# Larger clusters for the low-rank term: 12 token tiles at a time, with a second layout of V for two batches

## The chip, the cores and the metric

The kernel runs on one core of one Trainium2 chip. The metric is the device time of one execution in microseconds (us). The kernel before the change took 324.93 us (median of 3 runs, 324.88 to 324.94).

Engine names below: PE is TensorE's matmul side and PEld its weight load, DVE is VectorE, ACT is ScalarE, POOL is GpSimd, SP is SyncE, which here only issues DMAs. "L457" is line 457 of the kernel.

## What is computed

`x` has 8 batches of 4224 tokens with 192 channels. First a causal convolution of 7 taps along the tokens, with softmaxed taps per head (8 heads of 24 channels). On its result y a mixer block works:

```python
xt = x.transpose(0, 2, 1)                 # x is now the convolution's result, y
h = xt @ U @ V                            # rank 32, along the tokens
u = x + h.transpose(0, 2, 1)
ch = np.maximum(u @ w_ch1, 0.0) @ w_ch2   # 192 -> 768 -> 192
return (u + ch).astype(np.float32)
```

U is 4224 x 32 and V is 32 x 4224. All matrix work is done in bf16 with float32 sums.

## The kernel before

**Tiles and groups.** A token tile is 128 tokens. A batch has 33 tiles, so there are 264; eight tiles make a group, and there are 33 groups (`GT = 8`, `NG = 33`). As 33 is odd, the first tile of batches 1, 3, 5 and 7 has an odd number when tiles are counted through all batches. A group may hold tiles of two batches.

**The stages.**
- `conv32` (L321): the convolution of one batch as banded matmuls, a head at a time into two PSUM banks, evicted to `y_sb` by ACT and DVE (L256, L258). It reads x and a shifted copy `xb_sb` that POOL makes (`x_shift`, L293 to L305).
- `tt_mm`, `tt_split`, `tt_sum` (L396 to L435): the 32 x 192 product of U and y for one batch, in one PSUM bank. `tt_split` takes it out as a high part (`tt_hi`, ACT, L416) and a low part (`tt_lo`, DVE, L417), `tt_sum` adds up the column groups with two matmuls (L428) and DVE writes `tt_sb` (L422), copied into all four 32-partition row groups.
- `h_tiles` (L446): for a stretch of tiles of one batch, one matmul a tile (L457) of 32 rows of V by `tt_sb`, and on DVE the add u = y + h (L479). Tiles 2·pr and 2·pr+1 share one PSUM bank, and their matmul uses row group pr % 4. All matmuls of the first halves of the banks are issued first, then all of the second halves. One add covers both tiles of a bank if they lie in the same half group of four; otherwise there are two adds (L470). `h_group` (L488) calls this for the eight tiles of a group.
- `transp` (L496): the DMA transpose of a group of u into `uT`, issued on SP.
- `w1` (L542): a group's first product, 36 matmuls (L554) in 6 blocks of two banks, each block evicted with relu into `rl_sb` by ACT (L568) or DVE (L570). 
- `w2` (L577): two tiles' second product, 12 matmuls (L583) into one bank; DVE adds u and writes `out_sb` (L592), and SP sends it out (L600). There are four such pieces a group.

**PSUM.** All PSUM tiles come from one pool of eight banks (`psp`, `bufs=8`, one tag), taken in turn by `bank()` (L56). The banks for h are taken in the order in which `h_tiles` first meets them.

**The order of the work** is written by hand in `SLOTS` (L619 to L668), and every engine works through its own instructions in that order. A slot does w1 of its groups, then their w2 pieces, numbered p = 0, 1, ...; before piece p it does what `at[p]` lists: `c` a part of a convolution, `x` the shifted copy for the next batch, `t` and `s` the two steps of the U product, `h10` the h of group 10 and its transpose. Slots k = 5 to 13 come from a loop: each has three groups (12 pieces), and makes h for three groups further on, at p = 5, 8 and 11 (k = 5 to 9, where batch k-2 is convolved as well) or at p = 0, 4 and 8 (k = 10 to 12). In the profile, the slots with k = 5 to 13 begin at 81.16, 109.46, 137.40, 165.57, 193.59, 221.61, 246.48, 271.44 and 296.04 us.

**Loads.** x of batch b comes in four POOL DMAs during w1 (`x_load`, L610), with steps of `x_shift` between them (L794 to L806). V lies in `V_sb` (L711): partition block q holds tile pairs q, q+4, and so on; it is loaded by five POOL DMAs near the start (L715, L722).

Of the kernel before, what the change touches and what calls it, by code (L numbers as in the profile page):

```python
# [9 lines left out]
BF16 = mybir.dt.bfloat16  # L10
# [4 lines left out]
def kernel(  # L15
# [10 lines left out]
    nc = tc.nc  # L26
    P = nc.NUM_PARTITIONS
    B, S, D = x.shape
    H, KC = weight.shape
    GS = D // H  # L30
    R = moe_U.shape[1]
    M4 = moe_w_ch1.shape[1]
    NT = S // P
    MC = M4 // P
    assert (D, R, MC, S % P) == (192, 32, 6, 0)
    GT = 8
    NTT = B * NT
    NG = NTT // GT
# [6 lines left out]
    cst = ctx.enter_context(tc.tile_pool(name="cst", bufs=1))  # L45
# [10 lines left out]
    def bank():  # L56
        return psp.tile([P, 512], F32, name="ps", tag="ps")
# [45 lines left out]
    def iota(t, pattern, base, mul):  # L103
# [20 lines left out]
        out=Ur[:, 0:nfull, :], in_=U4[0 : nfull * P, :].rearrange("(k p) c -> p k c", p=P)  # L124
# [10 lines left out]
    for m0, m1 in ((0, 2 * P), (2 * P, M4)):  # L135
        for hf in range(2):
            nc.gpsimd.dma_start(
                out=W1_sb[HB * hf : HB * hf + HB, :, m0:m1],
                in_=moe_w_ch1[:, m0:m1].rearrange("(c k) m -> k c m", k=HB),
# [27 lines left out]
    for hh in range(2):  # L167
# [3 lines left out]
        out=dif[:], in0=dif[:], scalar1=rq[:, 0:1], scalar2=None, op0=ALU.add  # L171
# [5 lines left out]
        out=d_sb[:],  # L177
# [8 lines left out]
        out=hot[:],  # L186
# [6 lines left out]
        out=ident[:], in0=fp[:], scalar1=float(P), scalar2=None, op0=ALU.is_equal  # L193
# [9 lines left out]
        out=c_sb[:].rearrange("p k h -> p h k"),  # L203
# [5 lines left out]
    for hh in range(2):  # L209
        pr = sml.tile([P, KC, HQ, BW], BF16, name="pr")  # L210
        prs.append(pr)
        nc.vector.tensor_tensor(
            out=pr[:],
# [8 lines left out]
        out=Eq[:], in0=efp[:], scalar1=rq[:, 1:2], scalar2=None, op0=ALU.is_equal  # L222
# [3 lines left out]
        out=fp[:], in0=fp[:], scalar1=R - 1, scalar2=None, op0=ALU.bitwise_and  # L226
# [3 lines left out]
        out=R4[:], in0=fp[:], scalar1=0.0, scalar2=None, op0=ALU.is_equal  # L230
# [181 lines left out]
    def tt_split(b, p):  # L412

        hi = sml.tile([P, D], BF16, name="tt_hi")
        lo = sml.tile([P, D], BF16, name="tt_lo")
        nc.scalar.activation(out=hi[:], in_=p[:, 0:D], func=ACT.Copy)  # L416
        nc.vector.tensor_tensor(out=lo[:], in0=p[:, 0:D], in1=hi[:], op=ALU.subtract)  # L417
        ttb[b] += [hi, lo]
# [22 lines left out]
    def u_group(g):  # L441
        if ut[g] is None:
            ut[g] = us.tile([P, 4, 3, 2, HB], BF16, name="u_sb")
        return ut[g]

    def h_tiles(b, j0, j1):  # L446

        banks = {}
        for a in range(2):
            for pr in range(j0 // 2, (j1 + 1) // 2):  # L450
                j = 2 * pr + a
                if not j0 <= j < j1:
                    continue
                q = pr % 4
                if pr not in banks:
                    banks[pr] = bank()
                nc.tensor.matmul(  # L457
                    out=banks[pr][:, a * D : (a + 1) * D],
                    lhsT=V_sb[32 * q : 32 * q + 32, (j // 8) * 2 + j % 2, :],
                    rhs=ttb[b][32 * q : 32 * q + 32, :],  # L460
                    start=True,
                    stop=True,
                    tile_position=(32 * q, 0),
                )
        for pr in sorted(banks):
            js = [j for j in (2 * pr, 2 * pr + 1) if j0 <= j < j1]
            runs = []
            for j in js:
                t = b * NT + j
                if runs and t % 4 != 0:  # L470
                    runs[-1].append(j)
                else:
                    runs.append([j])
            for run in runs:
                n = len(run)
                t = b * NT + run[0]
                g, hf, i = t // GT, (t % GT) // 4, t % 4
                a = run[0] % 2
                nc.vector.tensor_tensor(  # L479
                    out=u_group(g)[:, i : i + n, :, hf, :],  # L480
                    in0=yt[b][:, run[0] : run[0] + n, :].rearrange("p n (c k) -> p n c k", c=3),
                    in1=banks[pr][:, a * D : (a + n) * D].rearrange(
                        "p (n c k) -> p n c k", n=n, c=3
                    ),
                    op=ALU.add,
                )

    def h_group(g):  # L488
        t0, t1 = g * GT, g * GT + GT
        while t0 < t1:  # L490
            b = t0 // NT
            te = min(t1, (b + 1) * NT)
            h_tiles(b, t0 - b * NT, te - b * NT)
            t0 = te

    def transp(g):  # L496
        uTt[g] = uts.tile([P, 4, 3, P], BF16, name="uT")
        return nc.sync.dma_start_transpose(
            out=uTt[g][:].rearrange("p i c t -> p (i c) t"),
            in_=ut[g][:].rearrange("p i c f k -> p (i c f k)"),  # L500
        )
# [100 lines left out]
    def held(ins, after):  # L602
        tc.add_manual_dep(
            ins.ins,
            after.ins.name,
            mybir.DependencyInfo(mybir.DependencyClass.Sync, mybir.DependencyReason.DATA),
            reason="transfer held back",
        )

    def x_load(b, q, after):  # L610
        if q == 0:
            x_tile(b)
            x_zero(b, nc.gpsimd)
        held(x_part(b, *XP[q]), after)
# [4 lines left out]
    SLOTS = [  # L619
        ([0], [], {}),  # L620
        ([1], [0], {0: ["h0"], 1: ["h3", "l2:2"], 2: ["l2:3"]}),
        ([2], [1], {0: ["d1", "h1"], 1: ["t1"], 3: ["s1"], 4: ["h4", "x2:6"]}),
        ([3], [2], {1: ["h5"], 3: ["h6"]}),
        (
            [4, 5],
            [3, 4, 5],
            {
# [8 lines left out]
            },  # L636
        ),
    ]
    nh = 10
    for k in range(5, 14):  # L640
        gs = list(range(3 * k - 9, 3 * k - 6))
        hs = [f"h{g}" for g in range(nh, min(nh + 3, NG))] + [None] * 3
        nh = min(nh + 3, NG)
        if k == 5:
            at = {
                2: ["c3:0:3:AAD"],
                3: ["c3:3:3:AAD"],
                4: ["c3:6:2:A", "x4:4"],
                5: [hs[0]],
                6: ["t3"],  # L650
                8: ["s3", hs[1]],
                11: [hs[2]],
            }
        elif k < 10:
            b = k - 2
            at = {
                0: [f"c{b}:0:2:A"],
                2: [f"c{b}:2:3:AAD"],
                3: [f"c{b}:5:3:AAD"] + ([f"x{b + 1}:4"] if b + 1 < B else []),
                5: [f"t{b}", hs[0]],  # L660
                7: [f"s{b}"],
                8: [hs[1]],
                11: [hs[2]],
            }
        else:
            at = {0: [hs[0]], 4: [hs[1]], 8: [hs[2]]}
        SLOTS.append((gs, gs, {p: [w for w in what if w] for p, what in at.items()}))
    assert nh == NG  # L668

    LOADS = {2: [(1, 5), (1, 5)], 3: [(4, 1), (4, 4), (5, 1), (5, 4)]}  # L670
    for b in range(4, B):
        g = 3 * b - 6
# [25 lines left out]
    o = 0  # L698
    for r, (k0, k1) in KP[2].items():
        j = NB0 // 2 * r + k0  # L700
        nc.gpsimd.tensor_copy(
            out=U4_sb[:, o : o + k1 - k0, :, :],
            in_=U_sb[:]
# [6 lines left out]
    NSL = (NT + 7) // 8 * 2  # L710
    V_sb = cst.tile([P, NSL, P], BF16, name="V_sb")  # L711
    full = NT // 8
    for q in range(4):
        src = moe_V[:, 0 : full * 8 * P].rearrange("r (k q t) -> r k q t", q=4, t=2 * P)
        nc.gpsimd.dma_start(  # L715
            out=V_sb[32 * q : 32 * q + 32, 0 : 2 * full, :].rearrange(
                "r (k a) t -> r k (a t)", a=2
            ),
            in_=src[:, :, q, :],
# [3 lines left out]
        out=V_sb[0:32, 2 * (NT // 8), :], in_=moe_V[:, (NT - 1) * P : NT * P]  # L723
# [32 lines left out]
    for r in range(4):  # L756
        q = slice(QB * r, QB * r + QB)
        for hh in range(2):
            nc.gpsimd.tensor_copy(
                out=band2[q, HQ * hh : HQ * hh + HQ, :],  # L760
                in_=bands[hh][q, :, HB * (r % 2) : HB * (r % 2) + QB],
            )

    def do(what):
        if what[0] == "c":
            b, h0, n, engs = what[1:].split(":")
            conv32(int(b), int(h0), int(n), engs)
            return
        if what[0] == "d":
            for h in range(H):  # L770
                last = conv(int(what[1:]), h, 1, [0, 1], "AA" if h == 2 else "AD")
            held(transp(3), last)
            return
        if what[0] == "l":
            b, q = (int(v) for v in what[1:].split(":"))
            x_load(b, q, done_w2[-1])
            return
        if what[0] == "x":
            b, n = (int(v) for v in what[1:].split(":"))
            steps.extend(x_shift(b))  # L780
            for _ in range(n):
                steps.pop(0)()
            return
        n = int(what[1:])
        if what[0] == "h":
            h_group(n)
            if n > 1 and n != 3:
                transp(n)
        elif what[0] == "t":
            tt_split(n, tt_mm(n, range(NT)))  # L790
        else:
            tt_sum(n)

    for gs1, gs2, at in SLOTS:  # L794
# [13 lines left out]
        for p in range(npc + 1):  # L808
            for what in at.get(p, []):
                do(what)  # L810
            if p < npc:
                g, k = gs2[p // 4], p % 4
# [35 lines left out]
```

## Time and profile before

| what | value |
|---|---|
| median of 3 runs | 324.93 us |
| span of the profiled execution, first to last instruction | 323.2 us |
| TensorE clock granted | 1.00 of full speed |
| busy: PE, DVE, ACT, POOL | 317.6, 268.6, 170.0, 142.7 us |
| L583 (w2) matmuls | 141.2 us busy, 1584 |
| L554 (w1) matmuls | 131.7 us busy, 1188 |
| L457 (h) matmuls | 12.4 us busy, 264 |
| L479 (u = y + h) on DVE | 168 adds: 96 of two tiles, mean 547 ns, and 72 of one tile, mean 347 ns |

The page is of one execution; its own time is the span and what lies around it, and the median is 1.7 us above the span. Matmuls are pipelined: the time of one (246 ns for L583) is longer than the distance between two starts, and the distances are what add up. The "chain" is the work that ended last, followed back from the end: at each step to what released an instruction, or to the one before it on its engine. A timeline row gives the start, the length and the engine; `x12` says that twelve instructions were merged, and square brackets tell how long the engine was idle before and for whom.

### The profile page before, as it was taken

What the parts mean: (1) busy time and instruction counts of PE and PEld (TensorE: products, weight loads), DVE (VectorE), ACT (ScalarE), POOL (GpSimd) and SP (SyncE); (2) the same over time, 40 slices, a digit from 0 to 9 for tenths busy, and PEclk for the clock granted to TensorE, in tenths of its full rate; (3) what the DMA queues carried; (4) which work ended last, traced back from release to release, by engine and by line L of the source; (5) the groups of instructions that cost most, each with busy time, mean ns of one, the idle gap of its engine ahead of it and who ended that gap; (6) DMA issues with size and microseconds to landing.
All of it is one profiled execution on the core that took longest, in us unless ns stands there. A gap on an engine that the chain in (4) does not pass through costs nothing.

```text
span 323.2 us, 9583 instructions
## 1 busy us (share of the span) xinstructions
PE 317.6 (98%) x3996; PEld 223.7 (69%) x3996; DVE 268.6 (83%) x551; ACT 170.0 (53%) x344; POOL 142.7 (44%) x111
## 2 busy tenths in 40 slices
PE   8999999999999999999999999999999999999995
PEld 3747676478677647866864884687797497487495
DVE  6769989987977986997898699789888897896863
ACT  1766724860874397088239609824903902912910
POOL 8764179728957983992897497000000000000000
PEclk9999999999999999999999999999999999999999
DMA  9999993999998999599499957138268059048035
GB/s 106 192 191 183 206 209 100 196 192 257 208 135 200 246 142 190 166 189 209 130 237 192 181 149 194 52 105 231 61 178 262 3 150 275 18 121 271 2 121 173
DMA packets 122906, 53.51 MB, mean 166 GB/s; under 512 B 87760, under 2 KB 122832, under 8 KB 122864
## 3 DMA queue, kind: packets, MB, share of 16 engines
q1 hardware_dynamic: 84528, 38.08, 45.4%
q0 software_dynamic: 38192, 14.73, 39.2%
q8 instruction: 31, 0.51, 0.7%
q10 hardware_dynamic: 144, 0.10, 0.1%
q14 instruction: 11, 0.09, 0.1%
HBM read 29.49 MB, written 25.95 MB: 172 GB/s over the span
## 4 chain that ended last, share of the span: by engine, by line
PE 92%; ACT 3%; DMA 2%; DVE 1%; issue 0%; POOL 0%; POOLq 0%
PE ps L583 42%; PE ps L554 39%; PE ps L339 3%; PE ps L457 3%; DMA x_sb<-in_x_dram 2%; PE ps L402 2%; ACT rl_sb L568 2%; PE ps L369 1%; ACT y_sb L256 1%; PE ps L509 1%; DVE u_sb L479 1%; DVE rl_sb L570 1%; PE ps L524 0%; PE ps L428 0%; POOL x_sb L79 0%
## 5 line engine op out<-in xcount | busy, mean ns | idle before, releaser
L568 ACT ACTIVATE rl_sb<-ps 128x512 bf16<-128x512 f32 x233 | 124.3, 604 | 108.0 <-PE ps L554 96.0
L583 PE MATMUL ps<-W_sb,rl_sb 128*128 128x192 bf16 x1584 | 141.2, 246 | 0.2
L583 PEld LDWEIGHTS <-rl_sb 128*128 128x128 bf16 x1584 | 128.3, 98 | 11.8 <-issue 11.5
L554 PE MATMUL ps<-uT,W_sb 64*128 64x512 bf16 x1188 | 131.7, 376 | 0.0
L570 DVE TENSOR_SCALAR rl_sb<-ps 128x512 bf16<-128x512 f32 x163 | 105.3, 688 | 15.7 <-PE ps L554 15.4
L554 PEld LDWEIGHTS <-W_sb 64*128 64x128 bf16 x1188 | 66.9, 94 | 60.4 <-issue 3.9
L592 DVE TENSOR_TENSOR out_sb<-ps,u_sb 128x384 f32<-128x384 f32 (+1 forms) x133 | 70.4, 551 | 25.5 <-PE ps L583 25.0
L305 POOL COPY xb_sb<-x_sb 32x3072 bf16<-32x3072 bf16 (+1 forms) x24 | 67.4, 2824 | 0.5
L479 DVE TENSOR_TENSOR u_sb<-y_sb,ps 128x192 bf16<-128x192 bf16 (+1 forms) x168 | 66.3, 461 | 0.0
L293 POOL COPY xb_sb<-x_sb 128x3072 bf16<-128x3072 bf16 x12 | 32.7, 2742 | 42.1 <-PE ps L339 32.2
L256 ACT ACTIVATE y_sb<-ps 128x384 bf16<-128x384 f32 (+4 forms) x90 | 38.3, 520 | 9.7 <-PE ps L339 7.4
L79 POOL DMA_DIRECT2D x_sb<-in_x_dram x32 | 27.0, 848 | 9.6 <-PE ps L457 3.8
L258 DVE CAST y_sb<-ps 128x408 bf16<-128x408 f32 (+4 forms) x36 | 19.1, 578 | 1.3 <-PE ps L369 1.0
L457 PE MATMUL ps<-tt_sb,V_sb 32*128 32x192 bf16 x264 | 12.4, 246 | 0.1
L339 PE MATMUL ps<-x_sb,band 64*32 64x384 bf16 x192 | 12.1, 333 | 0.0
L339 PE MATMUL ps<-xb_sb,band 64*32 64x384 bf16 x192 | 12.1, 332 | 0.0
L457 PEld LDWEIGHTS <-V_sb 32*128 32x128 bf16 x264 | 4.7, 92 | 7.3 <-issue 7.3
L416 ACT ACTIVATE tt_hi<-ps 128x192 bf16<-128x192 f32 x8 | 2.6, 330 | 11.9 <-PE ps L402 11.9
L369 PE MATMUL ps<-x_sb,band 64*64 64x240 bf16 (+3 forms) x192 | 8.0, 276 | 0.2 <-DMA x_sb<-in_x_dram 0.2
L339 PEld LDWEIGHTS <-band 64*32 64x32 bf16 x384 | 4.5, 89 | 5.2 <-issue 2.4
L153 PE MATMUL ps<-zz 128*128 128x512 f32 (+1 forms) x10 | 6.7, 816 | 1.1 <-DVE zz L143 1.1
L369 PEld LDWEIGHTS <-band 64*64 64x64 bf16 x192 | 6.0, 106 | 2.1 <-issue 1.4
(65 smaller groups left out, 71.3 us busy)
## 6 DMA issues: line engine op xcount, KB each, us to landing
out_dram<-out_sb SPq DMA_DIRECT2D x131, 192.0 KB, 2.7
x_sb<-in_x_dram POOLq DMA_DIRECT2D x14, 384.0 KB, 6.9
x_sb<-in_x_dram POOLq DMA_DIRECT2D x7, 432.0 KB, 6.7
x_sb<-in_x_dram POOLq DMA_DIRECT2D x7, 408.0 KB, 8.0
x_sb<-in_x_dram POOLq DMA_DIRECT2D x1, 504.0 KB, 7.3
uT<-u_sb SPq DMA_TRANSPOSE x31, 3.5
x_sb<-in_x_dram POOLq DMA_DIRECT2D x1, 480.0 KB, 5.6
W_sb<-in_moe_w_ch_dram POOLq DMA_DIRECT2D x2, 192.0 KB, 7.8
```

What stands on the lines that cost most here:

```text
L79: return nc.gpsimd.dma_start(out=xt[b][HB * r : HB * r + HB, s0:s1, :], in_=x[b, blk * HB : (blk + s1 - s0) * HB, :].rearrange("(j p) d -> ...
L256: nc.scalar.activation(out=out, in_=in_, func=ACT.Copy)
L293: nc.gpsimd.tensor_copy(out=xbt[b][:, s0:s1, :], in_=xt[b][:, s0 + 1 : s1 + 1, :])
L305: nc.gpsimd.tensor_copy(out=xbt[b][q, s0:s1, :], in_=xt[b][q, s0:s1, :])
L339: nc.tensor.matmul(out=pp[r][QB * cg : QB * cg + QB, 0 : nk[r] * GS], lhsT=w[hr], rhs=t[hr, st : st + 2 * nk[r] - 1 : 2, hs], start=True, ...
L457: nc.tensor.matmul(out=banks[pr][:, a * D : (a + 1) * D], lhsT=V_sb[32 * q : 32 * q + 32, (j // 8) * 2 + j % 2, :], rhs=ttb[b][32 * q : 32 ...
L479: nc.vector.tensor_tensor(out=u_group(g)[:, i : i + n, :, hf, :], in0=yt[b][:, run[0] : run[0] + n, :].rearrange("p n (c k) -> p n c k", c=3),
L554: last = nc.tensor.matmul(out=pps[m][hf][:], lhsT=W1_sb[HB * hf : HB * hf + HB, c, m * P : (m + 1) * P], rhs=uTt[g][HB * hf : HB * hf + HB ...
L568: nc.scalar.activation(out=rl[:, m, hf, :], in_=pp[hf][:], func=ACT.Relu)
L570: nc.vector.tensor_scalar_max(out=rl[:, m, hf, :], in0=pp[hf][:], scalar1=0.0)
L583: last = nc.tensor.matmul(out=cps[:, a * D : (a + 1) * D], lhsT=rlt[g][:, m, hf, (i + a) * P : (i + a + 1) * P], rhs=W2_sb[:, m, :], start ...
L592: nc.vector.tensor_tensor(out=o[:, 0:n, :].rearrange("p n (c k) -> p n c k", c=3), in0=cps[:, 0 : n * D].rearrange("p (n c k) -> p n c k", ...
```

## The change

For k = 5 to 12, h is no longer made group by group but for stretches of tiles (`w80:92` is tiles 80 to 91), two stretches a slot: 12 and 12 tiles (k = 5 to 9), or 10 and 12 (k = 10 to 12, as far as tiles are left). They stand at p = 5 and 9 (k = 6 to 9), at 6 and 10 (k = 5), and at 0 and 6 (k from 10). After a stretch, the groups that it completes are transposed. For batches 5 and 7, V is read from a second layout `Vo_sb` in which tiles 2·pr-1 and 2·pr stand together, so that a bank holds two tiles which lie in the same half group. `Vo_sb` is loaded by six POOL DMAs in slot k = 6, listed at p = 8, which POOL meets behind the four steps of `x5:4`.

```diff
     def h_tiles(b, j0, j1):
+        o, V = (1, Vo_sb) if b in odd else (0, V_sb)
         banks = {}
         for a in range(2):
-            for pr in range(j0 // 2, (j1 + 1) // 2):
-                j = 2 * pr + a
+            for pr in range((j0 + o) // 2, (j1 + o + 1) // 2):
+                j = 2 * pr + a - o
...
-                    lhsT=V_sb[32 * q : 32 * q + 32, (j // 8) * 2 + j % 2, :],
+                    lhsT=V[32 * q : 32 * q + 32, (pr // 4) * 2 + a, :],
...
-            js = [j for j in (2 * pr, 2 * pr + 1) if j0 <= j < j1]
+            js = [j for j in (2 * pr - o, 2 * pr + 1 - o) if j0 <= j < j1]
...
-    nh = 10
+    nt = 10 * GT
     for k in range(5, 14):
         gs = list(range(3 * k - 9, 3 * k - 6))
-        hs = [f"h{g}" for g in range(nh, min(nh + 3, NG))] + [None] * 3
-        nh = min(nh + 3, NG)
+        hs = []
+        for n in (12, 12) if k < 10 else (10, 12):
+            hs.append([f"w{nt}:{min(nt + n, NTT)}"] if nt < NTT else [])
+            nt = min(nt + n, NTT)
         if k == 5:
...
-                5: [hs[0]],
-                6: ["t3"],
-                8: ["s3", hs[1]],
-                11: [hs[2]],
+                6: ["t3"] + hs[0],
+                8: ["s3"],
+                10: hs[1],
...
-                5: [f"t{b}", hs[0]],
+                5: [f"t{b}"] + hs[0],
                 7: [f"s{b}"],
-                8: [hs[1]],
-                11: [hs[2]],
+                9: hs[1],
             }
+            if k == 6:
+                at[8] = ["v"]
         else:
-            at = {0: [hs[0]], 4: [hs[1]], 8: [hs[2]]}
+            at = {0: hs[0], 6: hs[1]}
...
+    odd = (5, 7)
+    Vo_sb = cst.tile([P, NSL, P], BF16, name="Vo_sb")
+
+    def v_odd():
+        for q in range(4):
+            k0 = 1 if q == 0 else 0
+            c0 = (8 * k0 + 2 * q - 1) * P
+            nk = full - k0
+            nc.gpsimd.dma_start(
+                out=Vo_sb[32 * q : 32 * q + 32, 2 * k0 : 2 * full, :].rearrange(
+                    "r (k a) t -> r k (a t)", a=2
+                ),
+                in_=bass.AP(
+                    tensor=moe_V.tensor,
+                    offset=moe_V.offset + c0,
+                    ap=[[S, R], [8 * P, nk], [1, 2 * P]],
+                ),
+            )
+        nc.gpsimd.dma_start(out=Vo_sb[0:32, 1, :], in_=moe_V[:, 0:P])
+        nc.gpsimd.dma_start(
+            out=Vo_sb[0:32, 2 * full : 2 * full + 2, :].rearrange("r a t -> r (a t)"),
+            in_=moe_V[:, (NT - 2) * P : NT * P],
+        )
...
+        if what == "v":
+            v_odd()
+            return
+        if what[0] == "w":
+            t0, t1 = (int(v) for v in what[1:].split(":"))
+            h_span(t0, t1)
+            for g in range(t0 // GT, t1 // GT):
+                transp(g)
+            return
```

`h_span(t0, t1)` is the loop of `h_group` over the batches that a stretch touches, with the ends given.

More of the change, by code (lines that the diff above doesn't have):

```diff
@@ L477, in h_tiles @@
                 g, hf, i = t // GT, (t % GT) // 4, t % 4
-                a = run[0] % 2
+                a = (run[0] + o) % 2
                 nc.vector.tensor_tensor(
@@ L486, in h_tiles, with h_span @@
                 )
-    def h_group(g):
-        t0, t1 = g * GT, g * GT + GT
+    def h_span(t0, t1):
         while t0 < t1:
@@ L494, in h_group @@
             t0 = te
+    def h_group(g):
+        h_span(g * GT, g * GT + GT)
     def transp(g):
@@ L659 @@
                 3: [f"c{b}:5:3:AAD"] + ([f"x{b + 1}:4"] if b + 1 < B else []),
-                5: [f"t{b}", hs[0]],
+                5: [f"t{b}"] + hs[0],
                 7: [f"s{b}"],
-                8: [hs[1]],
-                11: [hs[2]],
-            }
-        else:
-            at = {0: [hs[0]], 4: [hs[1]], 8: [hs[2]]}
-        SLOTS.append((gs, gs, {p: [w for w in what if w] for p, what in at.items()}))
-    assert nh == NG
+                9: hs[1],
+            }
+            if k == 6:
+                at[8] = ["v"]
+        else:
+            at = {0: hs[0], 6: hs[1]}
+        SLOTS.append((gs, gs, at))
+    assert nt == NTT
     LOADS = {2: [(1, 5), (1, 5)], 3: [(4, 1), (4, 4), (5, 1), (5, 4)]}
```

## The prediction

> **What bounds the kernel now.** I read the page's parts 1 and 4 first, then the chain in order of time, then the timelines of TensorE (PE), VectorE (DVE) and GpSimd (POOL) in one slot.
>
> ```profile
> PE 317.6 (98%) x3996; PEld 223.7 (69%) x3996; DVE 268.6 (83%) x551; ACT 170.0 (53%) x344; POOL 142.7 (44%) x111
> ...
> PE 92%; ACT 3%; DMA 2%; DVE 1%; issue 0%; POOL 0%; POOLq 0%
> ```
>
> PE is 92% of the chain: what is taken from PE's stream is gained, and what PE waits for is lost. DVE, at 83%, has little room to be late. Slot k=8 of the plan (165.57 to 193.59) shows a stretch that the change rewrites. PE's timeline there; the first number is when the first matmul of a group starts:
>
> ```profile
> 184.35 0.92 PE L402 MATMUL ps<-y_sb,U_sb 128*32 128x192 bf16 x33
> 185.20 0.34 PE L457 MATMUL ps<-tt_sb,V_sb 32*128 32x192 bf16 x8
> 185.48 2.15 PE L583 MATMUL ps<-W_sb,rl_sb 128*128 128x192 bf16 x24
> ...
> 187.63 1.15 PE L583 MATMUL ps<-W_sb,rl_sb 128*128 128x192 bf16 x12
> 188.72 0.42 PE L457 MATMUL ps<-tt_sb,V_sb 32*128 32x192 bf16 x8
> 189.07 3.14 PE L583 MATMUL ps<-W_sb,rl_sb 128*128 128x192 bf16 x36
> 192.15 0.34 PE L457 MATMUL ps<-tt_sb,V_sb 32*128 32x192 bf16 x8
> ```
>
> There is no idle time: each group follows the last. DVE in the same stretch, also without a gap after its first row:
>
> ```profile
> 185.67 0.36 DVE L417 TENSOR_TENSOR tt_lo<-ps,tt_hi 128x192 bf16<-128x192 f32 x1 [0.65 <-ACT tt_hi L416]
> 185.94 1.94 DVE L479 TENSOR_TENSOR u_sb<-y_sb,ps 128x384 bf16<-128x384 bf16 x4
> 187.80 1.02 DVE L592 TENSOR_TENSOR out_sb<-ps,u_sb 128x384 f32<-128x384 f32 x2
> 188.73 0.35 DVE L422 CAST tt_sb<-ps 128x192 bf16<-128x192 f32 x1
> 188.99 0.55 DVE L592 TENSOR_TENSOR out_sb<-ps,u_sb 128x384 f32<-128x384 f32 x1
> 189.46 2.00 DVE L479 TENSOR_TENSOR u_sb<-y_sb,ps 128x384 bf16<-128x384 bf16 x5
> 191.38 1.48 DVE L592 TENSOR_TENSOR out_sb<-ps,u_sb 128x384 f32<-128x384 f32 x3
> ```
>
> From the distances of the starts, DVE takes 0.465 for an add of two tiles or an output add (a result is ready 0.55 after its start), 0.26 for an add of one tile or a tt row (ready after 0.35).
>
> Does PE ever wait for such adds? Yes, in slot k=4, in the chain:
>
> ```profile
> 65.23 0.83 DVE u_sb L479 x3
> ...
> 66.22 1.08 DVE u_sb L479 x3
> ...
> 258.24 0.45 PE ps L457 x8
> ```
>
> All PSUM tiles come from one ring of eight banks, so an allocation waits for the reader of the one eight before it. In slot 4 the convolution's matmuls wait for the h adds. The last row (slot 11, right behind w1) is a cluster of 0.45 instead of 0.28: its fifth bank is held by a ScalarE relu that ends at 258.40 in ScalarE's timeline, and the matmul goes at 258.45. I take release = end of the reader + 0.05.
>
> **The change, part by part.**
>
> *Matmuls and breaks.* Eight tiles take 0.28 (185.20 to 185.48) or 0.35 (188.72 to 189.07). The matmuls of a cluster use four row groups, and one that needs a busy row group waits 0.08: counting the tiles of each group in the order of issue gives two waves for the 0.28 and three for the 0.35. Groups 10 to 32 are 23 clusters, four of them of three waves (12, 16, 20, 24): 23 x 0.28 + 4 x 0.08 = 6.76. Afterwards there are 16: 15 of four waves (0.44; six prs on four row groups, twice) and one of six (tiles 188 to 199, 0.60): 7.20. Loss 0.44. A w2 run cut in two costs 0.10 (12 matmuls alone 1.09, 36 take 3.08, so 0.995 per piece plus 0.10). Clusters that cut a run by themselves, and do not stand beside w1, tt or an earlier cut: 16 before, 8 after. Gain 0.80. Together -0.36.
>
> *DVE adds.* Carrying line 470's rule through both plans: 65 adds of two tiles and 54 of one become 81 and 22. 16 x 0.465 - 32 x 0.26 = -0.9 of DVE work. That is off the chain; it counts only through the banks. The old backlog into w1 is shorter too: slot 7's w1 is 11.92 against 11.76 elsewhere. -0.16.
>
> *Banks, slot 8, carried by hand.* First cluster, tiles 152 to 163: six banks, 185.20 to 185.64. Then p5 and p6 (1.99), s (0.16), p7 and p8 (2.08): the second cluster starts at 189.87. DVE: six adds 185.94 to 188.73, p5 188.73, p6 189.20, tt_sb 189.66, p7 189.92, p8 190.39, next adds 190.86. The second cluster, tiles 164 to 175, needs seven banks: eight allocations back lie three of the first cluster's, then p5, p6, s, p7. The seventh is p7's, free at 189.92 + 0.55 + 0.05 = 190.52. Its matmul stands in the middle: one more wave and the leaving (0.17) put the end at 190.78, not 190.31: **wait 0.47**. The next piece, p9, needs p8's bank: 190.39 + 0.60 = 190.99, **0.21** more. Slot 8: 0.68.
>
> The others by the same carry. Slot 5 (six banks, then seven): 0.68. Slot 6 (seven, then seven): p5 now takes the bank of tt, which tt_lo releases at 186.08 in slot 8's clock, while PE is there at 185.64: 0.44; three paired and six single adds take 2.96, so p7's bank comes at 190.69 and p8's at 191.16, against a cluster from 190.31: 0.20 + 0.21. Total 0.85. Slot 7 (seven, six): 0.44. Slot 9 (six, six): p9 waits 0.05. Sum 2.70. Before, all of these were zero: an 8-tile cluster has four or five banks, and the piece eight back had always been read.
>
> *Slots 10 to 12.* The first cluster stands right behind w1, with five or six banks. The fifth comes 0.275 after the start (258.17 to 258.45) instead of 0.08: 3 x 0.19. In slot 11 six banks are taken and the next piece needs that of the last relu, which ends at 258.89: 0.77 after the start against 0.63: 0.14. Before, slots 11 and 12 waited 0.17 and 0.19. Net +0.35.
>
> The Trainium skill pulls both ways here ("TensorEngine Tiling (Array Packing)"). Its section "Key Properties" says that a change of tiling mode drains TensorE: by that alone fewer clusters gain, as the -0.36 has it. Its "PSUM Pressure" says that row tiles write to different banks and that software must keep them apart, which speaks against seven banks at once: by that the +3.05 decides. The trace shows both prices, and the second is larger.
>
> *Vo and POOL.* Six more POOL DMA issues in slot 6, behind four x_shift steps. The nearest rows, V's own loads on line 715, take 0.54 each, and line 722's took 0.51: 4 x 0.54 + 2 x 0.51 = 3.2, with gaps 3.5. Queued behind them are x_load of batch 6 and the last two steps of x_shift(5), for which slot 7's first convolution (149.25) waits.
>
> ```profile
> 137.87 0.17 POOL L74 MEMSET x_sb<- 64x96 uint32 x1
> 138.49 0.82 POOL L79 DMA_DIRECT2D x_sb<-in_x_dram  x1 [0.45 <-PE ps L554]
> ...
> 142.85 3.08 POOL L305 COPY xb_sb<-x_sb 32x3456 bf16<-32x3456 bf16 x1
> ```
>
> The last step ends at 145.93. With 3.5 more, less the 0.45 that POOL sat idle, plus slot 5's delay (0.68 less about 0.25 of gains): 149.4. PE, itself late by slots 5 and 6 (1.53 less some 0.5 of gains), comes at 150.3. Cover 0.9: cost zero. If an issue takes as long as x's (0.82 to 0.86 each), some 1.7 more, PE waits about 0.8. The loads also add 0.27 MB written to DMA engines that are about full in slots 5 to 8; x of batch 6 lands later, by some 5 us at worst, and the cover in slot 8 (POOL done at 174.1, convolution at 177.26) shrinks to about one. Bounds: 0 to +1.2; I take 0, since V's rows are the same shape. On SP two transposes now stand together (1.44 each) before the outputs of p9 to p11; eight output buffers hold them through w1. Zero. Moving the second cluster to p9 leaves its groups at least a w1 pair (7.8) before use. Zero.
>
> Sum: -0.36 - 0.16 + 2.70 + 0.35 = **+2.5**. The profiled execution has a span of 323.2; the median of 324.93 lies 1.7 outside it, in what the change does not touch. 324.93 + 2.5 = **327.4**.
>
> **Rivals.** 1. *The banks come free in time* (not slower): if DVE ran some 0.9 ahead of my carry at p9 and the tt bank were free at p5, none of the 2.70 would arise and the late 0.35 stays at most; what remains is -0.36 - 0.16, about -0.5: 324.4. It decides from the point where p7's bank is free before the second cluster. For it: only the releases' order is inferred, not seen, in slots 5 to 9. Against it: slot 4's rows and slot 11's. 2. *POOL's cover is lost*: +1.2 on top, 328.6; for it, the full DMA engines. 3. *The second layout does not pair as meant* in batches 5 and 7: slot 9 would wait like slot 6 (0.85, not 0.05), and slots 11 and 12 some 0.3 for a further bank: +1.1, 328.5; against it, the index arithmetic gives 16 pairs in one bank each.
>
> **Chances.** Forecast 0.72, rival 1 0.13, rival 2 0.12, rival 3 0.03. The measurement tells about 0.2%, 0.65 us, from no change. Rival 1 lies within that, with a tail below: 0.09 of it same and 0.04 faster; 0.02 of the forecast's own chance is same, where the waits nearly vanish; the rest, 0.85, is slower. Range: the waits at half (1.5 of 3.05) give +1.0, 325.9, and I go a little below; rivals 2 and 3 reach 328.6. So 325.7 to 328.7; left out are rival 1 and a few hundredths at each end.
>
> **What would show it.** Right: in the chain after, u_sb L479, out_sb L592 and tt_lo L417 or waits of PE appear in w2 of slots 5 to 8 and hardly in 9; clusters of 12 at 0.44 where they do not wait; w2 runs unchanged between cuts; 152 adds on L479 instead of 168 (49 of the slots before 5, and 103). Wrong: the w2 parts of slots 5 to 8 no longer than before (rival 1), x_sb or xb_sb in the chain at slot 7's or 8's first convolution (rival 2), or clusters of 12 that take much more or less than 0.44.

## The result, and the profile after

The kernel after the change takes 327.15 us (median of 22 runs, 326.81 to 331.13) against 325.12 for the kernel before in the same rounds (22 runs). The ratio is 1.0065, with a 95% interval of 1.0046 to 1.0085; the medians differ by 2.0 us. The forecast was 327.4.

What follows rests on the traces. "Body" is the time from the first w1 matmul of slot 5 to the end of the last output add, "end" what follows up to the last instruction. The body leaves out the first 81 us, which the change does not touch and whose length moves by some 0.6 from execution to execution. Each body and each end is of one profiled execution. A slot that an edit does not touch agrees between kernels within 0.05; the one exception is slot 5 of e9.

| slot | before | after | difference |
|---|---|---|---|
| 5 | 28.30 | 28.73 | +0.42 |
| 6 | 27.94 | 28.75 | +0.80 |
| 7 | 28.17 | 28.30 | +0.14 |
| 8 | 28.02 | 28.55 | +0.53 |
| 9 | 28.02 | 28.09 | +0.06 |
| 10 | 24.87 | 24.90 | +0.03 |
| 11 | 24.96 | 25.04 | +0.08 |
| 12 | 24.60 | 24.89 | +0.29 |
| body (with slot 13) | 239.10 | 241.45 | +2.35 |
| end | 3.02 | 2.80 | -0.22 |

The page after, parts 1 and 4 (L480 is now the add of u, L557 and L586 the matmuls of w1 and w2, L595 the output add):

```profile
PE 318.0 (98%) x3996; PEld 220.4 (68%) x3996; DVE 268.5 (82%) x535; ACT 170.0 (52%) x344; POOL 146.1 (45%) x117
...
PE 85%; DVE 6%; ACT 4%; DMA 3%; issue 1%; POOL 0%; POOLq 0%
```

PE is 85% of the chain instead of 92%, and DVE 6% instead of 1%. PE's busy share is still 98%, so the busy share does not show the loss. PE's timeline in slot 8 does:

```profile
186.78 0.50 PE L458 MATMUL ps<-tt_sb,V_sb 32*128 32x192 bf16 x12
187.22 2.15 PE L586 MATMUL ps<-W_sb,rl_sb 128*128 128x192 bf16 x24
...
191.45 0.25 PE L458 MATMUL ps<-tt_sb,V_sb 32*128 32x192 bf16 x1
191.45 0.43 PE L458 MATMUL ps<-tt_sb,Vo_sb 32*128 32x192 bf16 x5
192.11 0.34 PE L458 MATMUL ps<-tt_sb,Vo_sb 32*128 32x192 bf16 x6 [0.23 <-DVE out_sb L595]
192.57 3.13 PE L586 MATMUL ps<-W_sb,rl_sb 128*128 128x192 bf16 x36
```

The first cluster of 12 takes 0.44 (186.78 to 187.22). The second takes 1.12 (191.45 to 192.57). Half way, six matmuls stand still for an output add on DVE. DVE there:

```profile
187.52 2.87 DVE L480 TENSOR_TENSOR u_sb<-y_sb,ps 128x384 bf16<-128x384 bf16 x6
190.31 1.02 DVE L595 TENSOR_TENSOR out_sb<-ps,u_sb 128x384 f32<-128x384 f32 x2
191.24 0.35 DVE L422 CAST tt_sb<-ps 128x192 bf16<-128x192 f32 x1
191.50 1.01 DVE L595 TENSOR_TENSOR out_sb<-ps,u_sb 128x384 f32<-128x384 f32 x2
```

Six adds hold DVE for 2.8; the output adds of p5 to p8 follow without a gap. p7's starts at 191.50 and ends 0.55 later, and the waiting matmul goes at 192.11. In slots 6 and 7, PE waits at once behind the first cluster; in slot 7:

```profile
158.48 0.50 PE L458 MATMUL ps<-tt_sb,V_sb 32*128 32x192 bf16 x12
159.36 2.14 PE L586 MATMUL ps<-W_sb,rl_sb 128*128 128x192 bf16 x24 [0.38 <-DVE tt_lo L417]
```

Seven banks are taken, so the next piece needs the bank of tt, which tt_lo still reads: 0.88 from cluster to piece instead of 0.44.

### The profile page after: what moved, and what is told of

The parts are those of the page before. It is cut to its first block, busy times and chain, and to the rows that moved or that the text cites. A ratio compares the mean times of both kernels' runs of the same rounds, so it can differ in the third digit from the quotient of the medians.

```text
span 325.6 us, 9583 instructions
## 1 busy us (share of the span) xinstructions
PE 318.0 (98%) x3996; PEld 220.4 (68%) x3996; DVE 268.5 (82%) x535; ACT 170.0 (52%) x344; POOL 146.1 (45%) x117
## 4 chain that ended last, share of the span: by engine, by line
PE 85%; DVE 6%; ACT 4%; DMA 3%; issue 1%; POOL 0%; POOLq 0%
PE ps L557 38%; PE ps L586 37%; PE ps L339 3%; DVE u_sb L480 3%; ACT rl_sb L571 2%; DMA x_sb<-in_x_dram 2%; DVE out_sb L595 2%; PE ps L458 2%; PE ps L402 2%; PE ps L369 1%; ACT y_sb L256 1%; PE ps L512 1%; DMA out_dram<-out_sb 1%; DVE rl_sb L573 1%; PE ps L527 0%
## 5 line engine op out<-in xcount | busy, mean ns | idle before, releaser
L586 PE MATMUL ps<-W_sb,rl_sb 128*128 128x192 bf16 x1584 | 139.8, 246 | 1.5 <-DVE tt_lo L417 0.8
L586 PEld LDWEIGHTS <-rl_sb 128*128 128x128 bf16 x1584 | 129.2, 98 | 11.6 <-issue 10.9
L557 PE MATMUL ps<-uT,W_sb 64*128 64x512 bf16 x1188 | 131.5, 376 | 0.0
L557 PEld LDWEIGHTS <-W_sb 64*128 64x128 bf16 x1188 | 61.2, 94 | 66.0 <-issue 3.1
L595 DVE TENSOR_TENSOR out_sb<-ps,u_sb 128x384 f32<-128x384 f32 (+1 forms) x133 | 70.0, 551 | 26.0 <-PE ps L586 25.6
L480 DVE TENSOR_TENSOR u_sb<-y_sb,ps 128x384 bf16<-128x384 bf16 (+1 forms) x152 | 64.7, 494 | 0.0
L458 PE MATMUL ps<-tt_sb,V_sb 32*128 32x192 bf16 x198 | 10.1, 246 | 0.4 <-DVE out_sb L595 0.2
```

The lines of the kernel that those rows point to most:

```text
L458: nc.tensor.matmul(out=banks[pr][:, a * D : (a + 1) * D], lhsT=V[32 * q : 32 * q + 32, (pr // 4) * 2 + a, :], rhs=ttb[b][32 * q : 32 * q + ...
L480: nc.vector.tensor_tensor(out=u_group(g)[:, i : i + n, :, hf, :], in0=yt[b][:, run[0] : run[0] + n, :].rearrange("p n (c k) -> p n c k", c=3),
L557: last = nc.tensor.matmul(out=pps[m][hf][:], lhsT=W1_sb[HB * hf : HB * hf + HB, c, m * P : (m + 1) * P], rhs=uTt[g][HB * hf : HB * hf + HB ...
L586: last = nc.tensor.matmul(out=cps[:, a * D : (a + 1) * D], lhsT=rlt[g][:, m, hf, (i + a) * P : (i + a + 1) * P], rhs=W2_sb[:, m, :], start ...
L595: nc.vector.tensor_tensor(out=o[:, 0:n, :].rearrange("p n (c k) -> p n c k", c=3), in0=cps[:, 0 : n * D].rearrange("p (n c k) -> p n c k", ...
```

## The experiments

All times are medians in us with the number of runs; the ratio is to the kernel before in the same rounds, with its 95% interval. The first row is of the first rounds; in the later ones the kernel before took 325.10 (with e2, e4, e6) and 325.16 (with e8, e9, e10).

| kernel | median (runs) | ratio | body | end |
|---|---|---|---|---|
| before | 325.12 (22) | 1 | 239.10 | 3.02 |
| after | 327.15 (22) | 1.0065 (1.0046 to 1.0085) | 241.45 | 2.80 |
| e1: no second layout | 329.43 (4) | 1.0121 (1.0089 to 1.0153) | 242.42 | 3.85 |
| e2: groups of eight, second layout | 324.57 (12) | 0.9978 (0.9956 to 1.0001) | 238.83 | 2.79 |
| e3: h before the U product | 329.02 (4) | 1.0120 (1.0065 to 1.0175) | 241.84 | 2.81 |
| e4: late clusters one piece later | 326.86 (12) | 1.0049 (1.0020 to 1.0077) | 241.09 | 2.80 |
| e5: second cluster later | 327.80 (6) | 1.0078 (1.0054 to 1.0102) | 241.73 | 2.80 |
| e6: groups placed by banks | 325.86 (12) | 1.0013 (0.9994 to 1.0032) | 238.82 | 3.77 |
| e7: four output pieces by ACT | 326.15 (10) | 1.0033 (1.0008 to 1.0057) | 240.27 | 2.81 |
| e8: e3, and s later | 325.86 (12) | 1.0012 (0.9992 to 1.0032) | 240.02 | 2.79 |
| e9: e6 with the second layout | 324.63 (12) | 0.9989 (0.9953 to 1.0024) | 239.17 | 2.80 |
| e10: before, four more DVE instructions | 326.43 (12) | 1.0041 (1.0013 to 1.0069) | 239.14 | 3.93 |

The diffs are against the kernel after, except for e10.

### e1: the stretches without the second layout

```diff
-                at[8] = ["v"]
+                pass
...
-    odd = (5, 7)
+    odd = ()
```

> Three theories for the 2.0 us that the change costs. Banks: PE waits for PSUM banks that DVE reads late. Load: the six loads of the second layout, on POOL and on full DMA engines. Waves: a cluster of 12 is dearer on PE by itself. Here the stretches stay and the second layout goes, with its loads. Banks: slot 9 then has seven banks in both clusters and should wait like slot 6 (0.89 in the trace after the change, instead of 0.06), slots 11 and 12 some 0.2 more for a further bank: about +1.0 on the changed kernel, 328.2. Load: the 2.0 go, 325.1. Waves: 327.1, or a little less, since fewer waves are needed at the end.

The body is 0.97 longer than after the change, where the banks asked for about 1.0. Slot 9 goes from +0.06 to +0.72 against the kernel before, slot 11 from +0.08 to +0.35. Slot 9 now has seven banks in both clusters:

```profile
215.23 0.50 PE L458 MATMUL ps<-tt_sb,V_sb 32*128 32x192 bf16 x12
216.11 2.14 PE L586 MATMUL ps<-W_sb,rl_sb 128*128 128x192 bf16 x24 [0.38 <-DVE tt_lo L417]
```

This cluster takes 0.88 up to the next piece, and so does the second (220.33 to 221.21). The loads are not what the change costs: without them the kernel is slower. The median moved by 2.3, more than the body: the end is 3.85 instead of 2.80. That was not in any theory, and e10 takes it up.

### e2: the second layout without the stretches

```diff
-        for n in (12, 12) if k < 10 else (10, 12):
+        for n in (8, 8, 8):
...
-                6: ["t3"] + hs[0],
-                8: ["s3"],
-                10: hs[1],
+                5: hs[0],
+                6: ["t3"],
+                8: ["s3"] + hs[1],
+                11: hs[2],
...
-                9: hs[1],
+                8: hs[1],
+                11: hs[2],
...
-                at[8] = ["v"]
+                at[8] = at[8] + ["v"]
...
-            at = {0: hs[0], 6: hs[1]}
+            at = {0: hs[0], 4: hs[1], 8: hs[2]}
```

> The other half of the change alone: groups of eight at their old places, with the second layout for batches 5 and 7 and its six loads. Banks: no cluster has more than five banks, nothing waits that did not before, DVE has a little less to do and the small waits at the starts of slots 10 to 12 shrink: 0 to 0.4 below the kernel before. Load: 2.0 above it, 327.1. Waves: as before.

The body is 0.27 shorter than before, mostly in slot 12 (-0.19, no bank wait behind w1); slot 8 is 0.07 shorter and slot 9 0.08 longer, which has to do with row groups (see the part on why the prediction was right). The median is 0.5 lower, and 0.2 of that is the end; the interval of the ratio still touches 1. The loads cost nothing that shows, the second layout is a small gain, and the loss of the change lies in the stretches.

### e7: output pieces evicted by ACT

```diff
-        nc.vector.tensor_tensor(
...
+        if 6 <= g < 21 and g * 4 + t0 // 2 - 12 * (g // 3) in (5, 6, 7, 8):
+            nc.scalar.activation(
+                out=o[:, 0:n, :].rearrange("p n d -> p (n d)"),
+                in_=cps[:, 0 : n * D],
+                func=ACT.Copy,
+            )
+        else:
+            nc.vector.tensor_tensor(
...
```

> The output pieces p = 5 to 8 of slots 5 to 9 are copied out of PSUM by ACT, without the addition of u, which is left out for these 20 pieces; everything else stays. ACT is idle there. Banks: what the second cluster waits for (the banks of pieces 5 to 8 and the adds behind which DVE reads them) is free at once: 0.69 + 0.45 + 0.69 + 0.06 = 1.9 less, 325.2; the 0.45 at the tt bank in slots 6 and 7 stay. Load and waves: 327.1.

The body is 1.18 shorter than after the change, with the same matmuls and the same loads. So the lateness of DVE's reads is the larger part of what PE waited for in the second clusters. I expected 1.9, and 0.7 stayed: 0.28 in slot 5 and 0.21 each in slots 6 and 8. In slot 5 the second cluster stands at p = 10, so the piece behind it needs the bank of p9, which DVE still read. Slot 8 shows what stayed with ACT:

```profile
190.51 0.50 PE L458 MATMUL ps<-tt_sb,Vo_sb 32*128 32x192 bf16 x11
191.16 1.07 PE L586 MATMUL ps<-W_sb,rl_sb 128*128 128x192 bf16 x11
```

The cluster no longer stops, but 0.65 passes to the next piece instead of 0.44. A cluster of seven leaves one bank, that of the piece just before it, and even at once an eviction takes about half a microsecond (0.49 on ACT here, 0.55 on DVE). This is a second mechanism beside DVE's backlog: the number of banks itself.

### e3 and e8: h before the U product

```diff
-                6: ["t3"] + hs[0],
+                6: hs[0] + ["t3"],
...
-                5: [f"t{b}"] + hs[0],
+                5: hs[0] + [f"t{b}"],
```

> The first cluster of a slot is put before the U product instead of behind it, nothing else. Banks: DVE starts its adds some 0.7 earlier, in time in which it waited for tt_hi, and the tt bank is no longer needed by the next piece. The 0.45 in slots 6 and 7 shrink to about 0.3 (tt now waits for the piece before), the 0.69 in slots 5 and 8 to about 0.3, the 0.45 of slot 6 to about 0.3: some 1.3 less than the changed kernel, 325.8. Load and waves: the same loads and the same waves, 327.1.

This failed: the body is 241.84, 0.4 longer than after the change. Its four runs lie between 327.50 and 330.33, and the profiled one took 327.50; I go by its trace, and why two of the four took 330.3 is open. The cluster waits did shrink to 0.28, where about 0.3 was expected. In their place PE now waits at s, 1.8 in all in slots 5 to 9; in slot 8:

```profile
189.01 0.25 PE L428 MATMUL ps<-tt_hi,R 128*128 128x192 bf16 x1
189.50 0.24 PE L428 MATMUL ps<-tt_lo,R 128*128 128x192 bf16 x1 [0.24 <-DVE tt_lo L417]
```

The second matmul of s starts 0.49 after the first instead of 0.08: tt_lo stands behind six adds on DVE and comes at 189.11. The same order that lets the adds start sooner makes tt_lo late. I had not asked who waits for the instruction that was passed. e8 puts s a piece later:

```diff
-                6: ["t3"] + hs[0],
-                8: ["s3"],
-                10: hs[1],
+                6: hs[0] + ["t3"],
+                9: ["s3"],
+                11: hs[1],
...
-                5: [f"t{b}"] + hs[0],
-                7: [f"s{b}"],
+                5: hs[0] + [f"t{b}"],
+                8: [f"s{b}"],
...
-                at[8] = ["v"]
+                at[8] = at[8] + ["v"]
...
-            at = {0: hs[0], 6: hs[1]}
+            at = {1: hs[0], 7: hs[1]}
```

> The order with h before the U product, mended where it failed: s a piece later, so that tt_lo, now behind six or seven adds on DVE, is done before s needs it; slot 5's second cluster at 11; the late clusters at p = 1 and 7. Banks: what stays is the wait of about 0.28 behind each cluster of seven banks, which leaves one bank to the next piece: five of them (slots 5, 6 twice, 7, 8), 1.4 in all. From the changed kernel 2.78 + 0.67 of waits go, 1.4 come back and 0.3 for three cuts: 1.7 below it, 325.4, 0.3 above the kernel before. If only DVE's lateness cost time, and not the number of banks, it would be 324.0. Load: 327.1.

The body is 240.02, 1.43 shorter than after the change (1.7 expected). Every cluster of seven banks takes 0.715 or 0.716 instead of 0.43 up to the next instruction, wherever it stands: PE is late by 0.28 there though DVE has no backlog. In slot 6, behind the first cluster:

```profile
128.47 0.50 PE L458 MATMUL ps<-tt_sb,V_sb 32*128 32x192 bf16 x12
129.19 0.90 PE L402 MATMUL ps<-y_sb,U_sb 128*32 128x192 bf16 x33 [0.22 <-DVE out_sb L595]
```

Slot 6's w1 is also 0.29 longer, since slot 5's second cluster, now at 11, sends its adds into it; that is the part by which the expectation was short. None of the placements tried lets the stretches beat the kernel before.

### e4: the late clusters one piece later

```diff
-            at = {0: hs[0], 6: hs[1]}
+            at = {1: hs[0], 7: hs[1]}
```

> In slots 10 to 12 the two clusters go to p = 1 and 7 instead of 0 and 6. Banks: the relu evictions behind w1 are done after one piece, so 0.17 + 0.33 + 0.17 of waiting goes, and a cut of the w2 run comes on top in each (0.10): net 0.3 to 0.4 below the changed kernel. Load and waves: 0.3 above it.

The body is 0.36 shorter than after the change, slots 10 to 12 take 24.82, 24.83 and 24.82, and the clusters there 0.431 and 0.434: no wait is left. The median is 0.3 lower.

### e5: the second cluster later

```diff
-                10: hs[1],
+                11: hs[1],
...
-                9: hs[1],
+                11: hs[1],
```

> The second cluster of slots 5 to 9 goes to p = 11, two pieces later in slots 6 to 9 and one in slot 5. Banks: its own wait goes, except that a seven-bank cluster leaves one spare bank and the piece behind it waits some 0.3; but DVE then carries the six or seven adds into w1, where its relus come late and PE waits there, 0.3 to 0.6 a slot: about +1.0 on the changed kernel, 328.2, with the waits in w1. The rival within this theory: time alone is what lacks, all waits of the second clusters go (1.9), 325.2. Load and waves: 327.1.

The body is 0.28 longer than after the change, the median 0.65 higher. The direction was right, the size (1.0) too large. The waits moved as the banks have it: w1 of slots 6 to 10 is 11.67 to 11.88 from first to last matmul, where it is 11.45 after the change. DVE at the end of slot 6 and the start of slot 7's w1, which begins at 138.34:

```profile
137.13 3.06 DVE L480 TENSOR_TENSOR u_sb<-y_sb,ps 128x192 bf16<-128x192 bf16 x9
...
140.57 4.26 DVE L573 TENSOR_SCALAR rl_sb<-ps 128x512 bf16<-128x512 f32 x7
```

The first relu on DVE comes 2.2 after the start of w1. More time between the clusters does not help, because DVE has to do the adds somewhere and the next stage needs it.

### e6 and e9: groups of eight at places chosen by the banks

```diff
-        for n in (12, 12) if k < 10 else (10, 12):
+        for n in (8, 8, 8):
...
-                6: ["t3"] + hs[0],
-                8: ["s3"],
-                10: hs[1],
+                5: hs[0],
+                6: ["t3"],
+                8: ["s3"] + hs[1],
+                10: hs[2],
...
-                5: [f"t{b}"] + hs[0],
-                7: [f"s{b}"],
-                9: hs[1],
+                5: hs[0] + [f"t{b}"],
+                7: [f"s{b}"] + hs[1],
+                10: hs[2],
...
-            at = {0: hs[0], 6: hs[1]}
+            at = {1: hs[0], 4: hs[1], 7: hs[2]} if k == 11 else {0: hs[0], 2: hs[1], 5: hs[2]}
```

e6 has this without the second layout (the edit of e1 as well), e9 with it.

> A version from the bank theory: groups of eight, no second layout, each put where the eight banks and DVE have room: the first before the U product at p = 5, the second with s at p = 7 (slot 5: 5, 8), the third at 10 instead of 11, and earlier in slots 10 and 12 (0, 2, 5) and one later in slot 11 (1, 4, 7). It takes away the waits that the kernel before still has: 0.16 in slot 7's w1, 0.08 in slot 10's, 0.17 and 0.19 behind w1: 0.3 to 0.6 below the kernel before, 324.4 to 324.8. Load and waves: as before, 324.9 to 325.1.

The body is 238.82, 0.28 shorter than before: slot 7's 0.16 in w1 is gone, slots 10 and 11 lose 0.07 and 0.06; slot 12 keeps its 0.19. Yet the median is 0.8 above that of the kernel before in its rounds, since the end is 3.77. With the second layout:

> Groups of eight at the places that the banks allow, now with the second layout and its loads. From the start of slot 5 to the last output add it should take what the same places took without it, less the shorter backlog in slots 10 to 12, some 0.1 to 0.3: about 238.6 against 239.1 of the kernel before. What follows the last add should be 2.8 and not 3.8, if that excess goes with the twelfth fetch of instructions on queue q14 and with a DVE program of over 705 instructions: here it is shorter by some fifteen. Together 324.4, some 0.6 below the kernel before. If the excess belongs to the places of the groups, it stays: 325.4.

The end is 2.80, as expected, and the median 324.63 against 325.16 in its rounds; the interval of the ratio (0.9953 to 1.0024) includes 1. The profiled execution lost 0.55 in slot 5's w1 behind a backlog of DVE that slot 4 left: an output add at 78.44 had waited 1.07 for an output DMA, where the same add in e2 waited 0.33 for its matmuls. Slot 4 is the same in both, so this is put down to that execution; from slot 6 on it is 0.5 shorter than the kernel before. e2 and e9 have the lowest medians of all; neither is shown to beat the kernel before.

### e10: four more instructions on DVE

```diff
     band2 = cst.tile([P, H, QB], BF16, name="band2")
+    spare = cst.tile([P, 1], F32, name="spare")
+    for v in range(4):
+        nc.vector.memset(spare[:], float(v))
```

> The kernel before, with four one-column memsets of a spare tile on DVE ahead of the first slot, and nothing else: its DVE program goes from 705 to 709 instructions. If the excess at the end goes with the length of DVE's program, the time behind the last output add goes from 3.0 to about 3.8 and q14 shows a twelfth fetch: 325.9 to 326.2. If not: 325.1, or 0.2 more for the memsets themselves.

The body is the same to 0.04, the end goes from 3.02 to 3.93, and the median is 1.3 above that of the kernel before in its rounds (325.16), some 0.4 more than the traces of the two explain. The DMA view of the end of e10 (318 us to the last landing) shows one fetch of instructions on queue q14 and later outputs:

```profile
q14 instruction: 1, 0.01, 0.9%
issues: line engine op xcount, KB each, median us to landing
out_dram<-out_sb SPq DMA_DIRECT2D x2, 192.0 KB, 2.6
out_dram<-out_sb SPq DMA_DIRECT2D x1, 96.0 KB, 2.9
out_dram<-out_sb ACTq DMA_DIRECT2D x1, 96.0 KB, 2.8
```

The same view of the kernel before has no q14 row:

```profile
out_dram<-out_sb SPq DMA_DIRECT2D x2, 192.0 KB, 1.9
out_dram<-out_sb SPq DMA_DIRECT2D x1, 96.0 KB, 1.7
out_dram<-out_sb ACTq DMA_DIRECT2D x1, 96.0 KB, 1.7
```

## Why the prediction was right

**What bounds the kernel.** Right: what PE waits for was lost one for one. The waits below, the cluster lengths and the cuts add up to each slot's difference within 0.03.

**Matmuls and breaks.** Clusters of four waves took 0.43 to 0.44 (0.44 predicted), the one of six waves 0.60 without its wait (0.60 predicted). That row groups make the waves has a test in e2. It has the same eight tiles in the same place as the kernel before, but the second layout gives tiles of batch 5 other row groups. In slot 8's second cluster the most used row group then has two tiles instead of three, and the cluster takes 0.28 instead of 0.36; in slot 9's third it has four instead of three, and the cluster takes 0.44 instead of 0.36, though it has one bank less. What holds is this count, and not that every matmul waits for its own row group: in slot 8's second cluster before, the row groups are used in the order 2, 3, 0, 2, ..., and the fourth matmul starts 0.02 after the first.

**Banks.** This was the step that decided, and it held cluster by cluster:

| where | predicted wait | measured |
|---|---|---|
| slot 5, second cluster and next piece | 0.68 | 0.69 |
| slot 6, piece behind the first cluster | 0.44 | 0.45 |
| slot 6, second cluster and next piece | 0.41 | 0.45 |
| slot 7, piece behind the first cluster | 0.44 | 0.44 |
| slot 8, second cluster and next piece | 0.68 | 0.69 |
| slot 9, second cluster | 0.05 | 0.06 |
| slots 10 to 12, behind w1 | 0.71 | 0.69 |

Measured is the distance from the cluster's first matmul to the next instruction, less 0.435 (0.596 in slot 9, 0.431 in slots 10 to 12). e7 shows the cause for the second clusters: with the output pieces evicted at once, 1.18 of 1.9 goes. e8 shows what stays when DVE has no backlog: 0.28 behind each cluster of seven. The carry had both in one number and did not tell them apart; DVE's lateness is some two thirds of the second clusters' waits, and the rest is the number of banks.

**DVE adds.** 152 as predicted. Slot 7's w1 lost its 0.16 and slot 10's its 0.08, of which the prediction had counted the first. It put the 0.16 beside the fewer adds; e6, which has no second layout and no fewer adds, loses it too, so the earlier place of slot 6's last cluster is enough.

**Vo and POOL.** Zero was right. From the start of the first to the end of the last, the six issues took 3.3 where 3.5 was expected:

```profile
138.42 2.26 POOL L777 DMA_DIRECT2D Vo_sb<-in_moe_V_dram x4
140.67 0.52 POOL L787 DMA_DIRECT2D Vo_sb<-in_moe_V_dram  x1
141.18 0.52 POOL L788 DMA_DIRECT2D Vo_sb<-in_moe_V_dram  x1
...
146.25 3.08 POOL L305 COPY xb_sb<-x_sb 32x3456 bf16<-32x3456 bf16 x1
```

The last x_shift step ends at 149.3 and the convolution starts at 150.5: a cover of 1.2, where 0.9 was carried. In slot 8, where it was feared to shrink to about one, it stayed at 3.2 (175.7 to 178.9).

**Total.** The body grew by 2.35 where 2.5 was predicted. By terms: waits 3.10 (3.05 predicted), cluster lengths +0.43 (0.44), breaks, read from the distances in w2 and s, -0.95 (-0.80), w1 -0.23 (-0.16). The breaks are the one term that was off by more than 0.1, and it came out in the change's favour. The end was 0.22 shorter, which the prediction left at nothing. Both bring 327.4 to 327.15 and a little below; the rest is within what the medians tell.

**The rivals.** The banks did not come free in time, POOL's cover held, and the second layout pairs: e1 against the kernel after is its worth in the stretches, 0.97, where the rival had 1.1.

## What to carry to other kernels

Before work is put into larger batches, carry the ring of buffers by hand: write down which allocation each new one replaces and when its reader is done, on the reader's own queue. A batch that takes all but one of the buffers makes the next step wait for the step just before it, even when the reader is idle (0.28 here for each cluster of seven banks), and a reader that is 83% busy turns a larger burst into a wait elsewhere (at the tt bank, at s, or in w1) when it is moved. Read PE's waits from the chain and the starts, not from its busy share, which stayed at 98%.

## What was not expected of the hardware

The end of the program, from the last output add to the last instruction, took 2.79 to 2.81 in the kernels with 662 to 695 instructions on DVE, 3.02 in the kernel before (705), and 3.77 to 3.93 in e1, e6 and e10 (707 to 708). In these three a fetch of 8 KB on q14 begins at 320.4 to 323.9, while the last outputs are on their way, and the last two of these land 0.9 to 1.2 later; in the kernel before, the last fetches begin at 323.5, behind everything. Four memsets early in the program are enough (e10). That DVE's program then needs one more block of instructions, and that its fetch holds up the outputs, fits the three cases but is inferred; the added instructions as the cause are shown. A difference of one microsecond between two versions can come from there and say nothing about the change: compare the body as well as the total.
